# Scores of four row tiles in one PSUM tile, Q copies on ScalarE, and a later chunk norm and QKV in a two-layer transformer kernel

## Chip, cores, metric

One core of one Trainium2 chip. The metric is the device time of one execution in microseconds (us), of which the profiled span is a little less (649.3 of 651.0 us in the profiled execution before).

## The reference

Two identical layers, each an attention block and a feed-forward block (FFN), each with a layer norm ahead and a residual add behind:

```python
# B, S, D = 1, 2048, 512; H = 32 heads of 16; W = 256; Dff = 1792; bf16
def _A_ref(x, wqkv, wo):                       # sliding-window attention
    qkv = (x @ wqkv) ...                       # [cut: reshape to q, k, v per head]
    scores = jnp.einsum("bhqd,bhkd->bhqk", q, k) * (Dh ** -0.5)
    mask = (idx[:, None] - idx[None, :] >= 0) & (idx[:, None] - idx[None, :] < W)
    p = softmax(where(mask, scores, -1e9))
    return einsum("bhqk,bhkd->bhqd", p, v) ... @ wo
def _B_ref(x, w1, w2):
    return jnp.maximum(x @ w1, 0) @ w2
x = x + _A_ref(_layernorm(x), wqkv, wo)
x = x + _B_ref(_layernorm(x), w1, w2)          # and the same two lines once more
```

## The kernel before

Rows are worked on in chunks of 512, with matmul results in PSUM tiles; two layers of four chunks make eight chunk steps (k = 0 to 7). A step has 20 slots, one for each of 4 head tiles x 5 groups of key blocks. Each slot issues the scores of one group, some nine dense 512-column matmuls, and, in four slots of five, the 24 small matmuls that multiply probabilities by V (PV). The dense matmuls come from a task list: FFN of an earlier chunk, output projection, and Q, K and V of the next chunk. Every engine is held to program order (a wrapper chains all instructions of an engine), so the slot in which something is issued decides what it stands behind.

The scores of a group, in two halves of two row tiles (32 rows = two heads of 16):

```python
ps_s = ... tile_pool(name="ps_s", bufs=2, space=PSUM)
def attn_half(layer, c, t, g, rp, Qt, pb):
    Sps = ps_s.tile([P, 2, 512], FP32, name="Sps")
    for kb, lo, n, at in blocks:
        for i in range(2):
            rows = slice(64 * rp + 32 * i, 64 * rp + 32 * i + 32)
            mm(Sps[:, i, 64 * at:64 * (at + n)], KBD[rows, t, sl]..., Qt[rows, 64 * lo:64 * (lo + n)], True, True)
    act.activation(pv4[:, 2 * rp:2 * rp + 2, ...], Sps[:, :, a:z], ACT.Exp, scale=0.25)
```

K goes by a ScalarE copy to a staging tile `Kst`, and from there by small DMA stores into a block-diagonal ring `KBD` of 20 slots. Eight stores serve a K tile; where the chunk wraps round the end of the ring (the chunks of steps 2 and 7, whose K is made in the step before) it takes sixteen. With `direct`, which only chunk 0 uses, VectorE writes the ring from PSUM and no store is needed:

```python
runs = [(0, 8)] if s0 + 8 <= NSLOT else [(0, NSLOT - s0), (NSLOT - s0, 8)]
...
if not direct:
    Kst = work.tile([P, 512], BF16, name="Kst", bufs=2)
    act.copy(Kst[:], ps[0][:])
for a, b in runs:
    for e in range(2):
        if direct:
            dve.tensor_scalar(out=KBD[:, t, sa:sa + b - a, e, :], in0=ps[0][...], scalar1=par[:, e:e + 1], ...)
            continue
        for r in range(4):
            nc.sync.dma_start(KBD[rows, t, sa:sa + b - a, e, :], Kst[rows, 64 * a:64 * b]...)
```

The same sync queue carries four stores per V tile and three kinds of DMA transpose: `OT` (attention output, read by the output projection), `xn2T` (its norm, read by the FFN), and `xnT` (the norm of the next chunk, read by Q, K, V). The schedule:

```python
def wo_done(k, j):                              # after the j-th output projection of a chunk
    if j % 2:
        ln_rows(c, xn2T[k], "B", j - 1, j + 1)  # FFN norm of two row tiles, then their transposes
    if j == 3:
        plan_ffn(k, now[0] + 3)
...
for k in range(NSTEP - 1):                      # norm of the next chunk, then its Q, K, V
    for j in range(4):
        at_slot(SPS * k + 1 + j, lambda k=k, j=j, fn=begin: fn(k, j))
    plan_qkv(k + 1, SPS * k + 6, SPS * k + 6, SPS * k + 19)
```

## Time and profile before

| | before |
|---|---|
| device time, 2 runs | 648.3 us (647.23 to 649.37) |
| profiled span, mean granted clock | 649.3 us, 0.888 |
| TensorE busy | 544.8 us |
| steps 3, 4, 5 (slots 60 to 120) | 70.4, 65.8, 69.0 us |

In the profile's lines PE is TensorE, PEld its weight loads, DVE VectorE, ACT ScalarE, POOL GpSimd and SPq the sync queue. L94 is the line of the wrapper, so go by tile names: `Sps` scores, `Pb` probabilities, `acc` the result of PV, `ps_d` that of any dense matmul, `x_sb` the residual rows, `xnA` and `xnB` the two norms before their transposes, `Vst` V before its stores. "Slot n" is counted over the run, 20 to a step.

A step is measured here from the start of the exponential of its slot 0 to that of the next step.

### The profile page before, as it was taken

The numbers are of one execution on the slowest core, as the hardware profiler recorded it, in microseconds if no ns is written. First come the engines' busy times: TensorE is split into PE (matmuls) and PEld (weight loads), VectorE is DVE, ScalarE is ACT, GpSimd is POOL, SyncE is SP. The second block draws the span as 40 slices with busy tenths as digits, with TensorE's granted clock in tenths as the row PEclk, the third lists the DMA queues.
The fourth block names the chain that finished last, engine by engine and source line by source line (L and its number), as shares of the span: only waits on it lengthen the run. The fifth ranks groups of instructions, "written<-read, shape, count | busy, mean of one in ns | idle before, by whom it ended". The sixth has DMA issues, their size and how long they took to land.

```text
span 649.3 us, 14626 instructions
## 1 busy us (share of the span) xinstructions
PE 544.8 (84%) x5644; PEld 241.2 (37%) x5741; DVE 352.6 (54%) x897; ACT 327.3 (50%) x355; POOL 255.0 (39%) x558
## 2 busy tenths in 40 slices
PE   5839766978979997999979997999796996997395
PEld 2213332433424443444424443444343343444142
DVE  5673444635565656565666566655662536643461
ACT  2335763654646665566545565666464556452000
POOL 6642363433453245533562255423542335321300
PEclk8678655997979999899989998999799897898788
DMA  8511223111222103211232123212311122001201
GB/s 278 208 33 24 39 40 50 26 26 27 42 51 42 36 9 67 46 37 22 41 64 39 26 41 61 37 31 51 65 31 24 25 50 59 2 17 35 48 1 38
DMA packets 101246, 30.65 MB, mean 47 GB/s; under 512 B 85552, under 2 KB 100656, under 8 KB 101168
## 3 DMA queue, kind: packets, MB, share of 16 engines
q1 hardware_dynamic: 101168, 29.63, 21.5%
q8 instruction: 47, 0.77, 0.5%
q14 instruction: 31, 0.25, 0.1%
HBM read 7.86 MB, written 2.10 MB: 15 GB/s over the span
## 4 chain that ended last, share of the span: by engine, by line
PE 58%; SPq 12%; DVE 11%; POOL 6%; DMA 5%; issue 4%; ACT 2%; DVEq 0%; POOLq 0%; ACTq 0%
PE ps_d L94 39%; PE Sps L94 10%; SPq L244 9%; PE acc L94 9%; DMA OT<-O 3%; POOL Pb L94 2%; SPq L266 2%; DVE stB L94 2%; ACT Pb L94 2%; DVE x_sb L94 1%; SPq L199 1%; POOL xnB L94 1%; POOL xnA L94 1%; DVE stA L94 1%; DMA V2f<-Vst 1%
## 5 line engine op out<-in xcount | busy, mean ns | idle before, releaser
L94 ACT ACTIVATE Pb<-Sps 128x1024 bf16<-128x1024 f32 (+2 forms) x320 | 307.7, 971 | 233.8 <-PE Sps L94 228.1
L94 POOL TENSOR_SCALAR_AFFINE_SELECT Pb<-Pb 64x256 bf16<-64x256 bf16 x368 | 153.4, 417 | 212.1 <-ACT Pb L94 193.6
L94 PE MATMUL ps_d<-xn2T,w 128*128 128x512 bf16 x421 | 117.5, 398 | 28.3 <-DMA xn2T<-xnB 14.1
L94 PE MATMUL Sps<-Qt,KBD 32*128 32x320 bf16 (+4 forms) x1408 | 125.9, 272 | 8.2 <-ACT Pb L94 5.6
L94 PE MATMUL ps_d<-w,hT 128*128 128x512 bf16 x420 | 107.0, 380 | 3.0 <-issue 1.3
L94 DVE TENSOR_SCALAR hT<-ps_d 128x512 bf16<-128x512 f32 x112 | 77.3, 690 | 51.7 <-PE ps_d L94 49.3
L94 PE MATMUL acc<-V2f,Pb 128*128 128x34 bf16 x2880 | 95.7, 180 | 2.8 <-DVE Pb L94 1.7
L94 PEld LDWEIGHTS <-KBD 32*128 32x128 bf16 x1408 | 42.4, 94 | 142.6 <-issue 138.9
L94 PEld LDWEIGHTS <-Pb 128*128 128x128 bf16 x2880 | 82.8, 97 | 28.3 <-issue 21.1
L94 PE MATMUL ps_d<-xnT,wqkv 128*128 128x512 bf16 x237 | 78.1, 429 | 12.7 <-DMA xnT<-xnA 9.4
L94 DVE RECIPROCAL chk<-acc 128x8 f32<-128x8 f32 x128 | 26.3, 206 | 80.4 <-PE acc L94 79.6
L94 PE MATMUL ps_d<-wo,OT 128*128 128x512 bf16 x114 | 38.7, 453 | 34.9 <-DMA OT<-O 33.0
L94 PEld LDWEIGHTS <-w 128*128 128x128 bf16 x448 | 39.2, 100 | 72.7 <-issue 41.0
L94 DVE TENSOR_TENSOR Pb<-Pb,tri 128x512 bf16<-128x512 bf16 (+1 forms) x152 | 60.0, 426 | 0.6 <-ACT Pb L94 0.6
L94 DVE TENSOR_TENSOR x_sb<-ps_d,x_sb 128x512 f32<-128x512 f32 x48 | 33.0, 689 | 47.7 <-PE ps_d L94 46.1
L94 PEld LDWEIGHTS <-hT 128*128 128x128 bf16 x448 | 36.8, 97 | 41.8 <-issue 8.3
L94 DVE CAST Vst<-ps_d 128x512 bf16<-128x512 f32 x28 | 19.4, 692 | 39.9 <-DMA V2f<-Vst 19.2
L94 DVE TENSOR_TENSOR O<-acc,chk 128x128 bf16<-128x128 f32 x128 | 37.3, 291 | 4.4
L94 POOL TENSOR_TENSOR rstdB<-rstdB,mhalf 128x2 f32<-128x2 f32 x16 | 12.1, 755 | 67.5 <-DVE rstdB L94 67.5
L94 PEld LDWEIGHTS <-wqkv 128*128 128x128 bf16 x256 | 22.8, 104 | 38.1 <-issue 24.7
L94 POOL TENSOR_TENSOR rstdA<-rstdA,mhalf 128x2 f32<-128x2 f32 x14 | 10.0, 714 | 63.0 <-DVE rstdA L94 62.9
L94 PE MATMUL ps_d<-wqkv,xnT 128*128 128x512 bf16 x119 | 33.6, 389 | 0.2
(65 smaller groups left out, 262.6 us busy)
## 6 DMA issues: line engine op xcount, KB each, us to landing
V2f<-Vst SPq DMA_DIRECT2D x112, 34.0 KB, 1.9
w<-in_B_w_dram SPq DMA_DIRECT2D x2, 1792.0 KB, 13.7
KBD<-Kst SPq DMA_DIRECT2D x160, 16.0 KB, 1.9
KBD<-Kst SPq DMA_DIRECT2D x128, 8.0 KB, 1.8
out_dram<-ob SPq DMA_DIRECT2D x16, 128.0 KB, 1.7
wqkv<-in_A_wqkv_dram SPq DMA_DIRECT2D x3, 512.0 KB, 7.5
xst<-in_A_x_dram SPq DMA_DIRECT2D x3, 512.0 KB, 9.4
xst<-in_A_x_dram SPq DMA_DIRECT2D x2, 256.0 KB, 3.0
```

The costliest lines, as they stand in the source:

```text
L94: inst = fn(*a, **k)
L199: nc.sync.dma_start_transpose(out=xnT[:, :, j * P:(j + 1) * P], in_=xn[:].rearrange("p (kc d) -> p kc d", kc=KC))
L244: nc.sync.dma_start(KBD[rows, t, sa:sa + b - a, e, :], Kst[rows, 64 * a:64 * b].rearrange("p (s k) -> p s k", k=64))
L266: nc.sync.dma_start(V2[64 * e:64 * e + 64, sl, e].rearrange("p a d -> p (a d)"), Vst[j % 2][64 * half:64 * half + 64, e].rearrange("p a d ...
```

## The change

The intent: half as many passages of TensorE into and out of a score block (0.10 to 0.12 us lost on each side of one in the trace before), half as many exponentials with their fixed cost (598, 705 and 1025 ns for 512, 640 and 1024 columns before, so 0.834 ns a column and, an estimate from these, 0.17 us fixed), VectorE relieved of the Q copies (0.69 us each), and a norm placed after the projections instead of before. The core of the diff (cut: the bookkeeping of masks, and a fallback path that does not run with these inputs):

```diff
-    ps_s = ctx.enter_context(tc.tile_pool(name="ps_s", bufs=2, space=bass.MemoryType.PSUM))
+    ps_s = ctx.enter_context(tc.tile_pool(name="ps_s", bufs=1, space=bass.MemoryType.PSUM))
-                dve.tensor_copy(Qt[:], ps[0][:])
+                (act.copy if chained[0] and not direct else dve.tensor_copy)(Qt[:], ps[0][:])
-    def attn_half(layer, c, t, g, rp, Qt, pb):
-        Sps = ps_s.tile([P, 2, 512], FP32, name="Sps")
-            for i in range(2):
-                rows = slice(64 * rp + 32 * i, 64 * rp + 32 * i + 32)
+    def attn_group(layer, c, t, g, Qt, pb):
+        Sps = ps_s.tile([P, 4, 512], FP32, name="Sps")
+            for r in range(4):
+                rows = slice(32 * r, 32 * r + 32)
-        act.activation(pv4[:, 2 * rp:2 * rp + 2, 64 + a:64 + z], Sps[:, :, a:z], ACT.Exp, scale=0.25)
+        act.activation(pv4[:, :, 64 + a:64 + z], Sps[:, :, a:z], ACT.Exp, scale=0.25)
-            at_slot(SPS * k + 1 + j, lambda k=k, j=j, fn=begin: fn(k, j))
-        plan_qkv(k + 1, SPS * k + 6, SPS * k + 6, SPS * k + 19)
+            at_slot(SPS * k + 5 + j, lambda k=k, j=j, fn=begin: fn(k, j))
+        plan_qkv(k + 1, SPS * k + 9, SPS * k + 9, SPS * k + 20)
```

More of the change, by code (lines that the diff above doesn't have):

```diff
@@ L207, in slot, with q_items @@
         return (32 * layer + kb) % NSLOT
-    def q_items(xnT, Qt, t):
+    def q_items(xnT, Qt, t, direct=False):
         ps = []
@@ L268, in v_items @@
         return [lambda kc=kc: one(kc) for kc in range(KC)]
-    def attn_half(layer, c, t, g, rp, Qt, pb):
+    def attn_group(layer, c, t, g, Qt, pb):
         first = c == 0
         blocks = [b for b in GROUPS[g] if not (first and b[0] < 0)]
-        Sps = ps_s.tile([P, 2, 512], FP32, name="Sps")
+        Sps = ps_s.tile([P, 4, 512], FP32, name="Sps")
         for kb, lo, n, at in blocks:
             sl = slot(layer, 8 * c + kb)
-            for i in range(2):
-                rows = slice(64 * rp + 32 * i, 64 * rp + 32 * i + 32)
-                mm(Sps[:, i, 64 * at:64 * (at + n)], KBD[rows, t, sl].rearrange("p e k -> p (e k)"),
+            for r in range(4):
+                rows = slice(32 * r, 32 * r + 32)
+                mm(Sps[:, r, 64 * at:64 * (at + n)], KBD[rows, t, sl].rearrange("p e k -> p (e k)"),
                    Qt[rows, 64 * lo:64 * (lo + n)], True, True)
@@ L459, in q_make @@
             Q[k, t] = work.tile([P, 512], BF16, name="Qt", bufs=5)
-            return q_items(xnTs[k], Q[k, t], t)
+            return q_items(xnTs[k], Q[k, t], t, k == 0)
         order = ["K0", "Q0", "V0", "K1", "V1", "Q1", "V2", "K2", "V3", "Q2", "K3", "Q3"]
@@ L544 @@
             force(s)
-            attn_half(layer, c, t, g, 0, Q[k, t], u % 2)
+            masks.append(attn_group(layer, c, t, g, Q[k, t], u % 2))
         for fn in events.pop(s, []):
@@ L548 @@
         done = run_tasks(s, -(-(budget + (3 if has_pv else 0)) // 2))
-        if len(masks) > 0:
+        if len(masks) > (1 if s < NS else 0):
             masks.pop(0)()
-        if s < NS:
-            masks.append(attn_half(layer, c, t, g, 1, Q[k, t], u % 2))
         if has_pv:
@@ L599, in exact_qblock @@
                 nc.vector.tensor_scalar_mul(qs, Qts[t][:, qc], hm[:, j:j + 1])
-                Sp = ps_s.tile([P, 2, 512], FP32, name="Sps")
+                Sp = ps_s.tile([P, 4, 512], FP32, name="Sps")
                 for i, kbi in enumerate(kbis):
@@ L615, in exact_qblock @@
                         sl = slot(layer, 2 * (qb - 2 + kbi) + half)
-                        trp = ps_s.tile([P, P], BF16, name="trp", tag="Sps")
+                        trp = ps_d.tile([P, P], BF16, name="trp", tag="ps_d")
                         nc.tensor.transpose(trp[hs, :], Pq[:, i * P + 64 * half:i * P + 64 * half + 64], ident[:])
```

## The prediction

> **What bounds the kernel now.** I read the page first (busy shares, slices, chain, groups), then the chain of waits of one steady stretch, then the timeline of that stretch by engine, and last the order in which the two built kernels issue their work on each engine.
>
> ```profile
> span 649.3 us, 14626 instructions
> PE 544.8 (84%) x5644; PEld 241.2 (37%) x5741; DVE 352.6 (54%) x897; ACT 327.3 (50%) x355; POOL 255.0 (39%) x558
> ...
> PE 58%; SPq 12%; DVE 11%; POOL 6%; DMA 5%; issue 4%; ACT 2%; DVEq 0%; POOLq 0%; ACTq 0%
> ...
> L94 ACT ACTIVATE Pb<-Sps 128x1024 bf16<-128x1024 f32 (+2 forms) x320 | 307.7, 971 | 233.8 <-PE Sps L94 228.1
> L94 PE MATMUL Sps<-Qt,KBD 32*128 32x320 bf16 (+4 forms) x1408 | 125.9, 272 | 8.2 <-ACT Pb L94 5.6
> ```
>
> PE bounds most of the span: 84% busy and 58% of the chain. ScalarE mostly waits for the scores (228 us), not the reverse (5.6 us). The rest of the chain, over a third, is the sync queue, VectorE, GpSimd and DMA landings, and that part decides this case.
>
> The loop has 160 slots, 20 per chunk step. A slot holds the scores of one group (two halves of two row tiles), about nine dense 512-column matmuls, and, in four slots of five, 24 small PV matmuls. The timeline of TensorE over half a slot:
>
> ```profile
> 300.50 0.81 PE L94 MATMUL ps_d<-xn2T,w 128*128 128x512 bf16 x3
> 301.24 0.39 PE L94 MATMUL Sps<-Qt,KBD 32*128 32x320 bf16 x6
> 301.56 1.47 PE L94 MATMUL ps_d<-w,hT 128*128 128x512 bf16 x5
> 302.96 0.39 PE L94 MATMUL Sps<-Qt,KBD 32*128 32x320 bf16 x6
> ```
>
> Six dense matmuls follow each other at 0.21 us. A half streams 512 columns on each of two row tiles, yet holds the array only 0.32 us (301.24 to 301.56): the two tiles run at the same time. Of these 0.32 us 0.21 are streaming and 0.11 are the switch back; another 0.10 to 0.12 us is lost going in (the last dense matmul before a half starts 0.31 us ahead of it instead of 0.21). A half costs 0.43 us.
>
> The second thing to see is the once-per-step stall. Timelines of VectorE, GpSimd and the sync queue around one:
>
> ```profile
> 397.00 0.69 DVE L94 TENSOR_TENSOR x_sb<-ps_d,x_sb 128x512 f32<-128x512 f32 x1 [2.45 <-PE ps_d L94]
> ...
> 399.34 0.17 DVE L94 TENSOR_SCALAR rstdB<-mvB 128x2 f32<-128x2 f32 x1
> ...
> 399.59 0.82 POOL L94 TENSOR_TENSOR rstdB<-rstdB,mhalf 128x2 f32<-128x2 f32 x1 [3.04 <-DVE rstdB L94]
> ...
> 401.10 1.52 POOL L94 TENSOR_SCALAR xnB<-x_sb,rstdB,nbB 128x512 bf16<-128x512 f32 x2
> 402.57 5.69 POOL L94 TENSOR_SCALAR_AFFINE_SELECT Pb<-Pb 64x256 bf16<-64x256 bf16 x12
> ...
> 389.96 2.50 SPq L199 DMA_TRANSPOSE xnT<-xnA  x2
> 392.63 1.19 SPq L346 DMA_TRANSPOSE OT<-O  x1
> 395.82 2.50 SPq L199 DMA_TRANSPOSE xn2T<-xnB  x2
> ```
>
> A transpose holds the sync queue 1.2 us and lands 2.4 to 2.5 us after its issue (the DMA view's median). Here the last OT transpose of the step sat behind two xnT transposes, and TensorE lost 3.8 us. The other lines time the norm ahead of the FFN: residual add to rstd 2.5 us, GpSimd to the end of the second row 3.0, then two transposes: add to landing 8.8 us. The 12 mask selects cost 0.47 us each.
>
> [...] 0.10 to 0.12 us lost on each side of a half, two tiles in the time of one. [...] no run here has four at once yet. [...] mean granted clock 0.888, with halved stretches of 3.4 to 6.8 us after these stalls. [...] the trace has 598, 705 and 1025 ns for 512, 640 and 1024 columns, which is 0.834 ns a column[...].
>
> **The change part by part.**
> (1) Scores. Two halves of 0.43 us become one block of about 0.43: 160 x 0.43 = 69 us of TensorE time, less for narrow groups of a first chunk, say 66 us. Regular slots run at 2.88, 3.41, 3.38, 3.36 and 3.41 us (mean 3.29), so they become 2.86, and 20 of them 57.2 us instead of 65.8.
> (2) Exponential. 272 of 1.025 us become 136 of 1.025 + 1024 x 0.000834 = 1.88; ScalarE saves about 0.17 x 160 = 25 us (narrow ones alike), takes 28 Q copies at 0.58 (16 us), and VectorE loses 28 x 0.69 = 19 us. None of this is on the path in regular slots. But the score tile now has one buffer: the next scores wait for about 0.45 (scores and hand-over) + 1.88 + 0.1 = 2.4 us. A slot of 2.86 hides that. The some 15 slots without dense work (steps 0 and 1, and 148 and 149) ran at 1.2 to 2.0 us and now need 1.6 to 2.7, about +8 us, which eats what (1) saves there.
> (3) The norm moves from slots 1-4 to 5-8, QKV from 6-19 to 9-20. Because every engine keeps program order, this is the large part. In the new order the sync queue takes per step OT, OT, OT, xn2T x2, OT, xnT x2, xn2T x2, xnT x2. Take the end of the second output projection as zero. Its residual add starts at 0.2; its xn2T transposes issue at 5.2 and 6.5; the last OT, now behind them, issues at 7.8 and lands at 10.2. TensorE has only 0.21 + 0.7 + 0.64 + 2.35 + 1.5 = 5.4 us of work before it needs that OT: 4.9 us stall. Then four dense matmuls and a PV, partly at half clock: 13.0. From there add 0.2, FFN norm to landing 8.8: 22.0; TensorE, with 5.5 us of work (two leftover slots), partly at half clock, gets to the first FFN matmul near 19.5: 2.5 us stall. The next chunk's norm comes after: rstdA on GpSimd starts when xnB is done (19.0), 1.3, then six mask selects 2.8, first xnA row 0.8, two issues 1.3 and landing 2.4: 27.7, where K's first matmul needs it. TensorE got there at 23: 4.8 us stall. The stretch takes 27.7 us instead of the 13.3 of its work: 14.4 lost, plus some 2.2 for the half clock after it. A full step is then 57.2 + 16.6 = 73.8 us; before it was 69.6 (slots 105 to 125).
>
> Over the run (working with positions in the order of issue):
> - start: the first xnT lands near 49 us in both, since GpSimd and VectorE set it. Slots 5 to 8 are run ahead meanwhile, then the ACT-bound slots and the first such stretch give it back: about level at 120 us.
> - step 2 wraps the K ring and issues 64 + 16 stores at 0.66 us, 53 us of sync queue from its first K copy on. That sets the time of the next OT in the new kernel (TensorE waits some 11 us) and nearly did before: 3 us ahead. Its stretch then takes 27.7 us where the old one took 9: 7.5 us behind at 206 us.
> - steps 3, 4, 5: +4.2 each: 20 us behind. Step 6 has a better queue order (OT before xn2T): -1.
> - step 7 wraps again, bound by the 53 us of stores in the new kernel, where the old one lost 5.9 us to a wait on V: -6, so about 13 behind. The tail with one FFN stall of 3 instead of 5 us: 10 to 11 behind, less a few us as the regular slots may overlap more than I count.
> Sum: 648.3 + 7 = 655 us.
>
> **The rivals.**
> (a) The saved array time reaches the end: 649 - 66 = 583 us, or about 600 with the old stalls. For it: PE is 84% busy and 58% of the chain, and OT0 to OT2 no longer sit behind xnT. Against it: the issue order, in which K's matmuls come two slots behind the norm's last apply, and OT3 behind xn2T; both waits are sums of durations above. If the stalls are half what I add up, five steps give back 35 us: 620 us.
> (b) ScalarE becomes the bound, one buffer and 1.88 us: every slot would then need about 2.4 us, less than the 2.86 of TensorE; it binds only slots without dense work. Alone it would leave about 595 us.
> (c) Four row tiles do not run at once[...]: the block costs 0.64 us and not 0.43, 34 us of the gain are gone, but the chains still cover part: about 670 us.
>
> **Range and chances.** The mean sits at +1%, with an uncertainty of about 2.5 us in each of six stretches (15 us if they err together), and 10 us for the start. 637 to 671 us for 8 in 10. Faster than 635.3: 0.15 (rival a); slower than 661.3: 0.32; between: 0.53.
>
> **What would show it.** Right: score blocks of 8 or 12 matmuls with 0.32 us to the next matmul, PE's time on Sps near half; exponentials of 1.88 us; PE waits for OT, xn2T and xnT of 2 to 5 us each in most steps, near 10 us each step together against 4 before; steps of some 74 us, and a granted clock under 0.888 with PE busy below 76%. Wrong: steps of about 62 us (the stalls are hidden, rival a); blocks of 0.5 us and more (rival c); long PE waits for ScalarE in regular slots (rival b).

## More of the kernel before

The final output tile `ob` shares the two buffers of `Kst`.

The page, the timelines and the stall of one step stand in the prediction. One view more, the waits of TensorE (columns: total us, how often, longest us), tells what interrupts it:

```profile
PE ps_d L94 <- DMA OT<-O: 33.0, 10, 5.2
PE ps_d L94 <- DMA xn2T<-xnB: 14.1, 2, 9.6
PE ps_d L94 <- DMA xnT<-xnA: 9.4, 1, 9.4
PE Sps L94 <- ACT Pb L94: 5.6, 13, 1.1
```

Of all TensorE's waiting (92.4 us), 56.5 us end with a transpose landing, chiefly OT. Two waits on V (`DVE Vst`), 10.4 us together, come next.

## The result and the profile after

The changed kernel took 674.17 us (2 runs, 673.61 to 674.74) against 648.3: ratio 1.0399, interval 1.0316 to 1.0482, slower. Ratios are the mean time of one kernel's fast runs over that of the other's fast runs of the same rounds, so not quite the ratio of the medians quoted. The output was correct. The time lies 3 us above the predicted range (637 to 671) and 19 above its centre.

The page of the changed kernel, the lines that answer to those in the prediction:

```profile
PE 507.5 (75%) x5741; PEld 239.7 (36%) x5741; DVE 333.7 (50%) x869; ACT 317.9 (47%) x223; POOL 253.3 (38%) x558
...
PE 46%; DVE 14%; SPq 12%; POOL 9%; DMA 9%; issue 5%; ACT 3%; DVEq 0%; POOLq 0%; ACTq 0%
...
L94 ACT ACTIVATE Pb<-Sps 128x2048 bf16<-128x2048 f32 (+2 forms) x160 | 283.4, 1771 | 207.4 <-PE Sps L94 193.3
L94 PE MATMUL Sps<-Qt,KBD 32*128 32x320 bf16 (+4 forms) x1408 | 67.2, 275 | 26.8 <-ACT Pb L94 25.8
```

TensorE's busy time fell by 37 us, that on the scores from 125.9 to 67.2, and yet the span grew: TensorE fell from 58% to 46% of the chain, and everything that hands data from one engine to the next (VectorE, GpSimd, DMA landings) grew. The granted clock fell to 0.844.

The score block itself did what was hoped. The timeline of TensorE around one (columns: start, us, engine, line, operation, count):

```profile
311.35 0.40 PE L94 MATMUL Sps<-Qt,KBD 32*128 32x320 bf16 x12
311.69 0.82 PE L94 MATMUL ps_d<-xn2T,w 128*128 128x512 bf16 x3
```

Twelve score matmuls on four row tiles hold the array from 311.35 to 311.69 (0.34 us; median of the regular blocks 0.33), hardly longer than six on two tiles did before (0.32 us).

The waits of TensorE, beside the list of before:

```profile
PE ps_d L94 <- DMA OT<-O: 48.9, 12, 10.5
PE ps_d L94 <- DMA xn2T<-xnB: 27.0, 7, 9.6
PE Sps L94 <- ACT Pb L94: 25.8, 22, 4.5
PE ps_d L94 <- issue: 18.3, 5, 4.6
PE ps_d L94 <- DMA xnT<-xnA: 15.0, 3, 7.6
```

Where they arise shows in one steady step. First TensorE (only lines with a wait, in brackets; the line with 0.25 us is left out), then the sync queue of the same stretch:

```profile
268.89 0.61 PE L94 MATMUL ps_d<-wo,OT 128*128 128x512 bf16 x1 [5.23 <-DMA OT<-O]
...
280.11 1.04 PE L94 MATMUL ps_d<-xn2T,w 128*128 128x512 bf16 x4 [2.76 <-DMA xn2T<-xnB]
285.70 1.01 PE L94 MATMUL ps_d<-xnT,wqkv 128*128 128x512 bf16 x2 [4.55 <-issue]
```

```profile
263.20 3.05 SPq L199 DMA_TRANSPOSE xn2T<-xnB  x2
266.41 1.19 SPq L346 DMA_TRANSPOSE OT<-O  x1
...
276.34 2.50 SPq L199 DMA_TRANSPOSE xn2T<-xnB  x2
281.89 2.50 SPq L199 DMA_TRANSPOSE xnT<-xnA  x2
```

Read the two together. The last OT is issued at 266.41, after two xn2T transposes, and lands 2.5 us later, when TensorE resumes (268.89). The second xn2T pair, issued from 276.34, ends the second wait at 280.11. The third wait is labelled "issue" because the trace joins no event to it. But the second of the two xnT transposes is issued at 283.17 and, at the usual 2.4 to 2.5 us, lands about 285.6, and the matmul that starts at 285.70 is the one that reads it: I read this wait as xnT's, and so most of the 18.3 us that the waits list calls "issue". The same three waits come in the next two steps: 4.89, 1.93 and 3.65 us, then 4.71, 1.20 and 4.59, the 3.65 us labelled as xnT's by the trace itself. Why xnT came so late, GpSimd tells:

```profile
275.54 1.52 POOL L94 TENSOR_SCALAR xnB<-x_sb,rstdB,nbB 128x512 bf16<-128x512 f32 x2
...
278.26 2.73 POOL L94 TENSOR_SCALAR_AFFINE_SELECT Pb<-Pb 64x256 bf16<-64x256 bf16 x6
281.10 2.00 POOL L94 TENSOR_SCALAR xnA<-x_sb,rstdA,nbA 128x512 bf16<-128x512 f32 x2
```

The next chunk's norm (xnA) now stands behind the FFN norm (xnB) and six mask selects: three chains that used to run side by side are in series. The windows of this step, before and then after (columns: window, its length, busy us and count for PE, PEld, DVE, ACT, POOL, then granted clock, DMA share, GB/s), put a size on it:

```profile
238.00:308.40 70.40, 65.40 (x738) 29.46 (x750) 42.17 (x108) 42.87 (x45) 31.32 (x68) 0.95 0.22 40
```

```profile
245.20:317.70 72.50, 59.26 (x749) 28.75 (x748) 40.10 (x104) 41.65 (x29) 31.28 (x68) 0.93 0.20 38
```

TensorE had 6.1 us less to do in that step, and idled 8.2 us more.

Starts of the steps (us from the start of the span) give the ledger of the whole run:

| | slot 20 | 40 | 60 | 80 | 100 | 120 | 140 | end |
|---|---|---|---|---|---|---|---|---|
| before | 84.8 | 165.8 | 238.0 | 308.4 | 374.2 | 443.2 | 521.4 | 649.3 |
| changed | 83.6 | 160.7 | 245.2 | 317.7 | 387.6 | 460.8 | 541.5 | 673.0 |
| changed − before | −1.2 | −5.1 | +7.2 | +9.3 | +13.4 | +17.6 | +20.1 | +23.7 |

The change is ahead until slot 40, loses 12.3 us in step 2, 2 to 4 us in each of steps 3 to 6, and 3.6 us after slot 140.

From slot 120 on the ledger parts from the prediction. There K and V of step 7 are stored, from step 6 into step 7. The sync queue from the first K store of the last chunk, before and then changed (most lines left out):

```profile
470.93 2.54 SPq L244 DMA_DIRECT2D KBD<-Kst  x4
...
517.62 10.75 SPq L244 DMA_DIRECT2D KBD<-Kst  x16
```

```profile
500.94 10.97 SPq L244 DMA_DIRECT2D KBD<-Kst  x16
...
546.14 10.96 SPq L244 DMA_DIRECT2D KBD<-Kst  x16
```

From the first store to the end of the last takes 57.4 us before (470.93 to 528.37) and 56.2 after: 64 K stores (43 to 44 us, 0.67 to 0.69 each) and 16 V stores, almost back to back; before, one xn2T pair of 2.5 us stands among them. The changed one starts it 30.0 us later and ends it 28.7 us later. TensorE meets this queue in two places: at a copy of V that waits for V's stores, and at the OT transposes issued behind the last store (before, then changed; lines between left out):

```profile
503.80 1.01 PE L94 MATMUL ps_d<-xn2T,w 128*128 128x512 bf16 x2 [5.56 <-DVE Vst L94]
...
540.88 1.04 PE L94 MATMUL ps_d<-wo,OT 128*128 128x512 bf16 x3 [0.84 <-DMA OT<-O]
```

```profile
532.00 1.01 PE L94 MATMUL ps_d<-xn2T,w 128*128 128x512 bf16 x2 [7.18 <-DVE Vst L94]
...
560.40 1.89 PE L94 MATMUL ps_d<-wo,OT 128*128 128x512 bf16 x4 [7.06 <-DMA OT<-O]
```

The first wait both kernels have. The second is 0.84 us before and 7.06 in the changed kernel, whose first OT is issued at 557.85, after the last store. VectorE stops too: the output tile `ob` takes a `Kst` buffer, so it waits for the last K stores to read theirs, 8.20 us before and 12.14 in the changed kernel, and VectorE, in order, stands still behind it. Before, this hardly reached TensorE, which had other matmuls to do and waited 0.59 us for `ob`.

### The profile page after: what moved, and what is told of

The parts are those of the page before. It is cut to its first block, busy times and chain, and to the rows that moved or that the text cites.

```text
span 673.0 us, 14446 instructions
## 1 busy us (share of the span) xinstructions
PE 507.5 (75%) x5741; PEld 239.7 (36%) x5741; DVE 333.7 (50%) x869; ACT 317.9 (47%) x223; POOL 253.3 (38%) x558
## 4 chain that ended last, share of the span: by engine, by line
PE 46%; DVE 14%; SPq 12%; POOL 9%; DMA 9%; issue 5%; ACT 3%; DVEq 0%; POOLq 0%; ACTq 0%
PE ps_d L94 35%; SPq L244 10%; PE acc L94 6%; PE Sps L94 5%; DMA OT<-O 4%; ACT Pb L94 3%; SPq L266 3%; DMA xnT<-xnA 3%; POOL Pb L94 3%; DVE stB L94 2%; POOL xnB L94 2%; DVE x_sb L94 2%; DVE stA L94 2%; POOL xnA L94 1%; DVE Pb L94 1%
## 5 line engine op out<-in xcount | busy, mean ns | idle before, releaser
L94 ACT ACTIVATE Pb<-Sps 128x2048 bf16<-128x2048 f32 (+2 forms) x160 | 283.4, 1771 | 207.4 <-PE Sps L94 193.3
L94 PE MATMUL ps_d<-xn2T,w 128*128 128x512 bf16 x448 | 131.6, 416 | 40.8 <-DMA xn2T<-xnB 27.0
L94 PE MATMUL ps_d<-w,hT 128*128 128x512 bf16 x448 | 115.9, 390 | 0.0
L94 PEld LDWEIGHTS <-Pb 128*128 128x128 bf16 x2880 | 94.0, 98 | 38.5 <-issue 14.1
L94 PE MATMUL ps_d<-xnT,wqkv 128*128 128x512 bf16 x256 | 80.9, 429 | 32.0 <-issue 16.4
L94 PE MATMUL Sps<-Qt,KBD 32*128 32x320 bf16 (+4 forms) x1408 | 67.2, 275 | 26.8 <-ACT Pb L94 25.8
L94 PE MATMUL ps_d<-wo,OT 128*128 128x512 bf16 x128 | 43.8, 470 | 48.9 <-DMA OT<-O 48.9
L94 DVE TENSOR_TENSOR Pb<-Pb,tri 128x512 bf16<-128x512 bf16 (+1 forms) x152 | 60.4, 430 | 6.7 <-ACT Pb L94 6.5
L94 PEld LDWEIGHTS <-KBD 32*128 32x128 bf16 x1408 | 25.4, 95 | 93.1 <-issue 90.2
L94 ACT CAST Kst<-ps_d 128x512 bf16<-128x512 f32 x28 | 16.3, 583 | 70.8 <-PE ps_d L94 63.9
L94 PE MATMUL ps_d<-wqkv,xnT 128*128 128x512 bf16 x128 | 36.9, 391 | 0.0
```

Of the source, the lines that this page charges most:

```text
L94: inst = fn(*a, **k)
```

## The experiments

Theory A (the prediction's): the score part pays, and the slot move (norm and QKV later) costs more than that, because it puts the OT, xn2T and xnT chains of a step in series. Rival B: the single score buffer makes TensorE wait for ScalarE (25.8 us now, 5.6 before). Rival C: the K stores on the sync queue are what makes the late slots costly, or what swallows the gain. (These are not the prediction's rivals, which have small letters. In the expectations A is theory 1, B theory 2, and the third theory is that the Q copies hold up the exponential; the "four-bank" scores there are those in the tile of four row tiles.) Every kernel below ran four times against runs of the kernel before on the same chip (medians of before 649.4 to 650.7 us), one of them twenty times.

**Old slots.** The changed kernel with the norm and QKV back in their old slots.

```diff
-            at_slot(SPS * k + 5 + j, ...)
-        plan_qkv(k + 1, SPS * k + 9, SPS * k + 9, SPS * k + 20)
+            at_slot(SPS * k + 1 + j, ...)
+        plan_qkv(k + 1, SPS * k + 6, SPS * k + 6, SPS * k + 19)
```

> The changed kernel with the norm back in slots 1 to 4 and QKV back in slots 6 to 19; four-bank scores and Q on ScalarE stay. Theory 1 (the moved slots cause the loss: three waits of 3 to 5 us a step on transposes in the queue's order): the waits on xn2T and xnT vanish, one OT wait of about 4 us a step stays, 600 to 615 us. Theory 2 (the single four-bank score buffer or the long exponential costs it): about 665 to 675 us as in the changed kernel. In steps 2 and 7 I expect the stores of K and V on the sync queue, some 55 us, to bind, so that not all of the 66 us are realised.

Measured: 617.8 us, ratio 0.9528 (0.9467 to 0.9589). The scores of four row tiles do pay, 32 us, and the slot move turns that gain into a loss of 26. Rival B falls here: TensorE's waits for ScalarE were 24.8 us in this kernel too. The value is a little above the expected 600 to 615: regular steps came to 60.1 to 63.9 us, but OT waits of 33.4 us remained.

**Slots only.** The kernel before with nothing but the slot move.

> The kernel before with only the norm in slots 5 to 8 and QKV in 9 to 20; half scores in two buffers, Q on VectorE. Theory 1: the same three waits a step (a little shorter, since TensorE brings more work along) on top of the old score cost: 695 to 720 us. Theory 2: within 1% of 648 us.

Measured: 709.37 us, ratio 1.093 (1.0871 to 1.0989), as expected. Its waits for OT, for xn2T and under "issue" are nearly those of the changed kernel (48.9, 27.0, 18.3), with the old score halves:

```profile
PE ps_d L94 <- DMA OT<-O: 45.8, 12, 10.8
PE ps_d L94 <- DMA xn2T<-xnB: 27.5, 6, 9.4
PE ps_d L94 <- issue: 18.3, 6, 4.0
```

**Scores only, and Q only.** The kernel before with the new score groups alone (Q still copied by VectorE), and with only the Q copy on ScalarE (the second line of the diff).

> Four-bank scores with one exponential alone; old slots, Q on VectorE. Theory 1: within 1% of the run with the old slots (600 to 615 us). Theory 2: 665 us or more. A third theory (Q copies on ScalarE hold up the exponential): clearly faster than the run with the old slots.

> Only the Q copies moved to ScalarE in the kernel before. Theories 1 and 2: within 1% of 648 us, since neither ScalarE nor VectorE is on the path of a regular slot. Third theory: over 2% slower.

Measured: 618.07 us, ratio 0.9512 (0.9457 to 0.9567), for the scores (as with the old slots, and like it above 615); 649.1 us, ratio 0.9999 (0.9979 to 1.0018, 20 runs), for Q, as expected. The Q copies are worth nothing either way. The parts add up: −32 (scores) + 0 (Q) + 60 (slots) = +28, against +26 for the whole change.

**Norm back, QKV still late.** The changed kernel with only the norm back in slots 1 to 4.

```diff
-            at_slot(SPS * k + 5 + j, ...)
+            at_slot(SPS * k + 1 + j, ...)
```

> The changed kernel with the norm back in slots 1 to 4, QKV left in 9 to 20. It splits the loss of 56 us between the two moves. My reading: K's wait on xnT (4 to 5 us a step) goes, the wait on xn2T (2 to 3 us) stays because nothing but leftovers of the second FFN product stands ahead of it, and the last OT waits behind xnT as in the kernel before. About 640 us, so the norm's move would be some 34 us and QKV's some 22. If the order behind xn2T alone mattered: 618 to 625. If only the late QKV mattered: 665 to 675.

Measured: 655.58 us, ratio 1.0083 (1.0052 to 1.0114). So of the 56 us between the changed kernel and the old slots, the norm's move is 18.6 and that of QKV 37.8, taken in this order (the norm moved with QKV already late); the other order was not run. I had expected about 640, that is, the norm to be the larger part: a miss. In the sync queue the last K stores of a chunk now stand in the next step, ahead of its first OT and xnT; and with QKV starting three slots later, TensorE has less else to do while it waits: OT waits were 60.4 us in total here, more than in the changed kernel.

**Half the stores.** The changed kernel with only the first run of K stores in the two wrapping steps, 8 per tile instead of 16. Wrong result on purpose (relative error 0.28).

```diff
-            for a, b in runs:
+            for a, b in runs[:1]:
```

> The changed kernel with one run of K stores left out in steps 2 and 7 (8 stores a K tile instead of 16; wrong numbers on purpose). If the sync queue's issue of stores binds these two steps, the waits of TensorE there (10.6 and 5.1 us in step 2, 7.6 and 7.4 in step 7) fall by about 20 to 25 us in all: 648 to 655 us. If the queue only trails other work: within 1% of 674.

Measured: 639.54 us, ratio 0.9819 (0.977 to 0.9869): 34.6 us less than the changed kernel had in its own rounds, above the 19 to 26 that I expected. By the starts of steps 16.3 us came by slot 60 (the first wrap) and 17.1 between slot 120 and the end (the second). So the stores do set the pace of both wrapping steps.

**Earlier norm; earlier norm and QKV.** If late is bad, is early good? Old slots with the norm at slots −2 to 1, and that with QKV in slots 3 to 17 as well.

```diff
+            at_slot(max(SPS * k - 2, 1) + j, ...)
+        plan_qkv(k + 1, SPS * k + 6, SPS * k + 6, SPS * k + 19)      # early_norm
+        plan_qkv(k + 1, SPS * k + 3, SPS * k + 3, SPS * k + 17)      # early_both, for k > 0
```

> A version meant to beat both: four-bank scores, Q on ScalarE, QKV in 6 to 19, and the norm of the next chunk two slots before the step begins (slots -2 to 1), so that its transposes are out of the queue before the first OT. The OT wait of 4 to 5 us in the regular steps should fall to about 1: 598 to 606 us. If something else holds OT: 615 to 620 as with the old slots.

> The same with QKV in slots 3 to 17 from step 1 on. The K stores of step 7 (and 2) start three slots, some 9 us, earlier: 588 to 600 us if the sync queue binds there; equal to the early norm alone otherwise.

Measured: 614.51 us, ratio 0.9454 (0.9411 to 0.9498), and 687.16 us, ratio 1.0569 (1.0535 to 1.0604). The first missed its 598 to 606 us: it gained 3 us on the old slots, with overlapping intervals. OT waits fell from 33.4 to 22.7 us, but waits for xn2T rose from 15.9 to 24.4. The second, expected at 588 to 600, is the worst miss and the most telling run. Its sync queue in a steady step:

```profile
268.10 5.99 SPq L244 DMA_DIRECT2D KBD<-Kst  x8
274.20 1.21 SPq L346 DMA_TRANSPOSE OT<-O  x1
...
279.17 10.12 SPq L244 DMA_DIRECT2D KBD<-Kst  x15
289.39 2.53 SPq L199 DMA_TRANSPOSE xn2T<-xnB  x2
```
QKV early means K stores early, and now these stand ahead of the last OT and of the second xn2T pair, which is issued at 289.39 behind fifteen stores. TensorE's waits for xn2T came to 68.7 us, from 24.4 with only the norm early. So Rival C is half right: late slots do not need the stores to be costly (the runs below show it), but the stores are a block of 5 to 6 us (10 when two tiles queue up) that any transpose issued behind them inherits.

**K without stores.** To take the stores away without a wrong result, VectorE writes the ring from PSUM as it does for chunk 0: once in the wrapping steps only (with the earlier norm, and on the kernel before), once in every step (with the earlier norm, and on the changed kernel).

```diff
-  lambda n=n: k_items(layer, c, xnTs[k], n, k == 0))
+  lambda n=n: k_items(layer, c, xnTs[k], n, k in (0, 2, 7)))   # early_direct_wrap, before_direct_wrap
+  lambda n=n: k_items(layer, c, xnTs[k], n, True))             # early_direct_all, changed_direct_all
```

> The version with the early norm, and in steps 2 and 7 K is written into its ring by VectorE from PSUM (4 writes of 256 columns or fewer a K tile) instead of 16 stores on the sync queue. If the queue of stores is what is left of the loss in these steps, TensorE's waits there (7.1 and 5.9 us in step 2, 8.0 and 5.4 us in step 7) go: 585 to 595 us. If VectorE's extra 7 us a step land on the path instead: 605 to 615 us.

> The same with K written by VectorE in every step. The remaining wait of about 2.6 us a regular step on xn2T should go too, since three or four K stores of 0.63 us stand ahead of those transposes in the queue: 572 to 588 us. If xn2T waits on the norm itself, not on the queue: equal to the run with VectorE in steps 2 and 7 alone.

> The kernel before with K written by VectorE in steps 2 and 7 alone. It tells how much of the time before was already the queue of stores: 630 to 640 us if the waits on V (5.3 and 5.9 us) and the lag of the following OT go; within 1% of 649 us if the two steps were bound by TensorE.

> The changed kernel, slots as changed, with K written by VectorE in every step, so that the queue's stores of K are out of the account. What is left against the version with the early norm and the same K (569.7 us) is the moved slots alone. If the three chain waits a step (about 5 on OT, 2 to 3 on xn2T, 4 to 5 on xnT, with the half clock after them) are what the slots cost, it is 620 to 640 us. If the slots cost time only through the queue of K stores, it is 570 to 590 us.

Measured:

| kernel | us | ratio to before (95%) |
|---|---|---|
| early norm, no stores in the wrapping steps | 582.1 | 0.8968 (0.8941 to 0.8994) |
| early norm, no stores at all | 569.74 | 0.8758 (0.8725 to 0.8792) |
| before, no stores in the wrapping steps | 631.64 | 0.9736 (0.9699 to 0.9773) |
| changed, no stores at all | 630.15 | 0.9687 (0.9647 to 0.9726) |

All four are correct. The first two came out a little under what I expected (585 to 595 and 572 to 588), the other two within it. The second beats both kernels: 12% faster than before. VectorE makes 80 such writes, 72 more than before (0.75 or 0.48 us each, 47.0 us in all), and is 64% busy. The window of a step (step 2, slots 40 to 60), columns as before:

```profile
152.00:212.00 60.00, 57.08 (x753) 28.17 (x753) 43.94 (x112) 39.45 (x25) 31.04 (x69) 1.00 0.19 37
```
TensorE is busy 57.1 of 60.0 us, at a granted clock of 1.00. Its waits for OT are down to 14.9 us in the whole run. The regular step without stalls that the prediction worked out, 57.2 us, is there: steps 80 to 100 took 57.0.

Four pairs of runs settle what belongs to what.

| us | old or early slots | late slots | late − old |
|---|---|---|---|
| score halves, K by stores | 648.3 (before) | 709.4 | +61 |
| score groups, K by stores | 617.8 (old slots) | 674.2 (changed) | +56 |
| score groups, K by stores | 614.5 (norm early) | 674.2 (changed) | +60 |
| score groups, K by VectorE | 569.7 (norm early) | 630.2 | +60 |

Late slots cost 56 to 61 us whether K is stored by DMA or not, and with either form of the scores. So Rival C falls as an explanation of the slot move, and theory A stands: the waits remain when the stores are gone. Without K stores TensorE waits 30.9 us for OT, 30.1 for xn2T, 15.1 for xnT and 17.5 under "issue" with the late slots, and 14.9, 18.8, 9.0 and none with the early norm; the difference is 51 of the 60 us. How much of it is the series of chains and how much the other work missing meanwhile was not taken apart. The stores are a second cost: 44 to 45 us with either set of slots, measured with the score groups. The kernel before pays it too, but for it only the wrapping steps were measured, 18 us.

## Why the prediction was wrong, point by point

- **Score block (part 1): right.** 0.33 us to the next matmul against 0.32 before, TensorE's time on Sps 67.2 from 125.9 (predicted: near half). That four row tiles would take no longer than two was the estimate: no trace showed four at once before this run. What makes up the 0.10 to 0.12 us on each side of a block was not shown. Rival (c) falls.
- **Exponential and Q copies (part 2): right.** 160 exponentials take 283.4 us, 24.3 less (predicted 25), and the Q copies change nothing. Waits for ScalarE rose by 20 us where I had counted about 8, but the kernel with old slots has them too and is 5% faster. Rival (b) falls.
- **The stretch of three stalls (part 3): right, in order and size.** Predicted 4.9, 2.5 and 4.8 us for OT, xn2T and xnT; measured 5.23, 2.76 and 4.55 in step 3, and 4.9, 1.9, 3.7 and 4.7, 1.2, 4.6 in steps 4 and 5. Predicted +4.2 us for each of steps 3 to 5; measured +2.1, +4.1 and +4.2. Slots 0 to 60: predicted "7.5 us behind at 206 us", measured 7.2 at slot 60. This match is partly luck: the line as printed (3 ahead, then 27.7 us against 9) would give 15.7 behind, and the measured course was 5.1 ahead at slot 40, 10.6 behind at slot 52, 7.2 behind at slot 60. The lower clock around the stalls is there too: a mean of 0.844 from 0.888, and in step 3 a granted clock of 0.50 from about 268.3 to 271.7 us and from 282.0 to 288.8, where TensorE resumes from stalls at 268.89 and 285.70. Rival (a) falls: times below 600 us came only without late slots and without stores in the wrapping steps.
- **The failed step: the sum after slot 120.** The prediction said "step 7 wraps again, bound by the 53 us of stores in the new kernel, where the old one lost 5.9 us to a wait on V: -6, so about 13 behind", then "10 to 11 behind, less a few us as the regular slots may overlap more than I count". Up to slot 120 the predicted sum was 20 behind and the measured 17.6. From there I let the changed kernel regain 9 to 10 us and took another 3 to 4 off for slots that might overlap; it lost 6.1 instead. The runs show why. The wait on V that I counted against the old kernel alone (5.56 us in the trace) the changed kernel has too (7.18 us). And the changed kernel enters that queue 30.0 us later though it was only 17.6 behind at slot 120: its first K store of the last chunk comes in slot 129, not 126, since norm and QKV were moved back. So its first OT of step 7 stands behind the last store, and TensorE waits 7.06 us for it, where the old kernel waits 0.84 for an OT. The runs without these stores give the size. From slot 120 to the end the kernel before takes 206.1 us, and 196.4 without them (before_direct_wrap); the changed kernel takes 212.2, and 195.1 with only half of them (changed_half_stores) or 194.1 with no K store at all (changed_direct_all). So the block costs the old kernel 9.7 us there and the changed one at least 17.1: 7 to 8 us more, where I had counted 6 less. (Each figure is from one profiled execution. The 194.1 also lacks eight stores of the chunk before, which the changed kernel issues after slot 120.) I knew the changed kernel to be bound by these stores, yet charged a wait to the old one alone; the changed one pays that wait too, and a second one.
- **The same error from the other side.** The score gain that I sized at 66 us of TensorE time showed as 32 us in the old slots. Without the stores of the two wrapping steps the distance between the kernel with score halves (631.6) and the one with score groups (582.1) is 49.5 us; the latter also has the earlier norm, worth 3.3 us in the runs with stores, so about 46. This comparison changes two things, so I call the remaining 14 us (46 − 32) a reading and not shown: that much of the score gain is waited away at the stores. It is near the size of the miss in step 7 and the tail. The store cost itself is shown: 18 us for the kernel before (the run without these stores), and 34.6 for half of them in the changed one.
- **Slips that changed nothing.** The OT wait of 3.8 us in the prediction's example is that of the weight loads; TensorE's matmuls waited 3.57.
- **What stays open.** Why QKV's three to one slots of delay cost twice the norm's four (37.8 against 18.6 us) I explain by the order in the sync queue and by missing other work for TensorE; no run took the two apart. Both moves together cost 60 us with no K store in the queue, which speaks for the missing work.

## What to carry to other kernels

Where engines and a DMA queue execute in order, list for each landing that TensorE waits for what stands ahead of it in its queue, and what other work TensorE has until then, before moving anything by a few slots: moving norm and QKV later cost 56 to 61 us here, and moving QKV earlier 73, though no work was added. Count the issue time of small DMAs as busy time of an engine (64 K stores took 43 to 44 us of one wrap), and ask of each version where it will wait for such a block: the one that reached it later waited more here (7.18 and 7.06 us against 5.56 and 0.84). When a saving on the busiest engine moves the time little, take the next chain out as well: score groups alone gave 32 us, with norm order and stores repaired the same groups stand in a kernel 79 us faster.

## What the runs show of small DMAs and row tiles

- Small K stores (8 and 16 KB): 0.64 to 0.69 us of sync queue for most of them, against 1.8 to 1.9 us from issue to landing. Moving all of them to VectorE took 44 to 45 us off.
- One small DMA transpose within SBUF, 128 x 512 bf16: 1.2 to 1.3 us of queue for most and 2.4 to 2.5 us from issue to landing.
- Score blocks: 0.10 to 0.12 us lost on each side of one (0.31 us from the last dense matmul to the block, and 0.33 for the block itself, where 512 columns take 0.215). Four tiles of 512 columns held the array 0.33 us with the loss on leaving in it, and two tiles 0.32. At that 0.215 us (median from one dense matmul of 512 columns to the next) one tile after the other would take 0.86, an estimate, so four at once took 2.6 times less; without the loss (0.22 us, also an estimate) it would be 3.9.
